# An inverse transform table built later and two groups of additions issued earlier, in a state-space and SwiGLU block kernel

## The chip, the cores and the metric

The kernel runs on one core of one Trainium2 chip. The metric is the device time of one execution, in microseconds (us); below it is called the timed value. The span in a profile, from the first to the last instruction, is about 1.8 us shorter.

## The reference

One batch of 2048 tokens with 640 channels. Condensed below. It is a block of two parts, each behind a layer norm: a state-space convolution whose kernel K is built from 192 complex exponentials per channel and applied by Fourier transform, and a SwiGLU feed-forward part with 1536 hidden channels.

```python
P = jnp.exp(logdA[:, :, None] * l[None, None, :])          # (D, N, L)
K = jnp.einsum("dn,dnl,dn->dl", Cc, P, dB).real
Yf = rfft(pad(u)) * rfft(pad(K)); y = irfft(Yf)[..., :L] + u * Dskip
...
h  = x + A(layernorm(x))
h2 = h + (silu(layernorm(h) @ w1) * (layernorm(h) @ w3)) @ w2
```

## The kernel before

Two parts of it matter.

**The building of K** (about 0 to 100 us of the span). The channels go in three chunks (256, 256 and 128). For each chunk VectorE and ScalarE make two tables, `at` and `bt`. ScalarE contributes sines, cosines and exps; VectorE multiplies them (`b_mul`). TensorE multiplies the tables (`k_mm`), ScalarE takes the product out of PSUM (`k_evac`, tile `kc`), TensorE transforms it (`k_dft`), and ScalarE takes out the result (`kf_evac`, tile `kf`). The inverse table `gt` with its negated copies is made by four transposes and four ScalarE copies; the second of these copies makes `nft`, a negated part of the forward table. `nft` is first used at 84.8 us, `gt` at 91.6 us.

```python
def inverse_table():
    tp = ps2("g", BF16)
    for i in range(NFT):
        T.transpose(out=tp[:, 0, i * P:(i + 1) * P], in_=ft[...], identity=ident[:])
    S.copy(out=gt[:], in_=tp...)          # L168
    S.mul(out=nft[:]..., mul=-1.0)        # L169
    S.mul(out=gn2[:], ..., mul=-1.0)      # L170
    S.mul(out=gn[:], ..., mul=-1.0)       # L171
...  (cut)
zs1 = z_sin(1)
at1 = a_first(1, wv1)
inverse_table()
run(a0)                                    # VectorE: end of the chain of table at, chunk 0
stg = [b_rest(0, bt0, "exp", ig) for ig in IGS]     # ScalarE: exps, L280; an exp table load comes first
for ig, st in zip(IGS, stg):
    b_mul(0, bt0, "exp", ig, st)           # VectorE: bt = bt * stg, L319
warm(14, last_a(0, at0)); warm(10, last_b(0, bt0, 1))
ze1 = z_exp(1)
bt1 = b_tile(1)
b_first(1, bt1, "exp")
ze2 = z_exp(2)
...  (cut)
pk = k_mm(0, at0, bt0, 0)                  # L373
...
k_evac(0, pk, kc, 0)
run(a_chain(1, at1, zs1))
pb = k_dft(0, kc)                          # L422
...
kf_evac(0, pb, "SSSS")                     # L439
for b in range(n_mm(1)):
    k_evac(1, k_mm(1, at1, bt1, b, (lambda: warm(6, idle, "g")) if b else None), kc, b)   # kc: L408
...
warm(6, idle)
pb = k_dft(1, kc); kf_evac(1, pb, "SSSS")
for part in range(2):
    fwd(0, SPLIT[0], part)                 # L576
...
pk = k_mm(2, at2, bt2, 0)                  # "the third chunk's k_mm"
```

`warm` issues matmuls without a use, meant to keep TensorE's clock up.

**The eight periods** (from 100 us). Each handles 256 tokens, by a string of steps that gives the program order. `Gi` is a pair of gate and up products (L853) with their evacuations `sg` and `up`, `Hi` the VectorE product of the two (L865). `I0`, `I1` are inverse transforms, `A0`, `A1` the additions that make h for the next period (L759 to L767), `T` its layer norm statistics (variance on VectorE, the power on POOL), and `X` its normalization (`xl`, L820), the store of it to DRAM (`xd`) and a DMA transpose back (`xt`). The next period's `G0` needs `xt`.

```python
PERIODS = ["p p G0 u1 p p H0 u2 u3 k G1 H1 I0 G2 H2 A0 I1 G3 H3 A1 T s0 G4 H4 s1 G5 X H5 L D s2 s3 K O0 B0 q0 q1 Y0 O1 ...", ...]
```

## Time and profile before

| | value |
|---|---|
| timed, 3 runs | 276.61 us (276.31 to 277.1) |
| the profiled execution | timed 276.8 us, span 275.0 us |
| busy share of the span: PE, DVE, ACT | 82%, 80%, 72% |
| DVE and ACT busy, 34 to 64 us (of 30 us) | 29.50 and 29.98 us |
| first gate matmul of period 0, of period 1 | 100.22 us, 122.40 us |

These are the page's engine shares, and the busy tenths of 40 slices of 6.9 us each. PEclk is the granted clock in tenths.

```profile
PE   7550165204789999999999999999999999999995
...
DVE  6999999999999989898879897797897886731112
ACT  6999999999998988856765774783693662642441
...
PEclk9555559555999999999999999999999999999999
```

VectorE and ScalarE fill the slices up to the 13th (about 86 us), TensorE those after the 14th. Next come two stretches of the first regime, from the view by windows: each engine's busy time with its count of instructions.

```profile
34.00:64.00 30.00, 10.81 (x533) 7.16 (x532) 29.50 (x35) 29.98 (x79) 0.00 (x0) 0.61 0.15 32
64.00:86.00 22.00, 17.06 (x665) 12.58 (x665) 21.41 (x41) 21.90 (x67) 3.34 (x9) 0.89 0.02 4
```

After the window and its length come PE, weight loads, VectorE, ScalarE and POOL, then the granted clock and the DMA. Only 0.5 and 0.6 us of VectorE's time are idle, and still less of ScalarE's. One of its idle stretches is in the timelines of ScalarE (first) and VectorE (second): start, duration, line, and in brackets the idle time before it and what ended it.

```profile
29.38 0.60 ACT L168 COPY gt<-ps_420 128x512 bf16<-128x512 bf16 x1
...
30.73 1.28 ACT L280 ACT_TABLE_LOAD   x1
32.02 3.42 ACT L280 ACTIVATE stg<-alp_182 128x384 bf16<-128x384 f32 x8
```

```profile
32.04 1.83 DVE L357 TENSOR_TENSOR at<-at,tt 128x1536 bf16<-128x1536 bf16 x2
34.23 2.16 DVE L319 TENSOR_TENSOR bt<-bt,stg 128x3840 bf16<-128x3840 bf16 x1 [0.36 <-ACT stg L280]
```

The four table copies (the first is shown, the last ends at 30.72) stand ahead of the exp table load, and VectorE waits 0.36 us for the exps behind it. The end of this regime, in TensorE's timeline, is the third chunk's k_mm. It waited for VectorE's last `bt`; TensorE had been idle for 0.17 us before it:

```profile
85.49 0.38 PE L576 MATMUL ps_1924<-uln_1755,nft 128*128 128x512 bf16 x1
86.04 1.96 PE L373 MATMUL ps_1934<-bt,at 128*64 128x64 bf16 x128 [0.17 <-DVE bt L319]
```

The second regime has one hole, before period 1. These are VectorE's and then TensorE's timeline, and the landing time of the one transpose in that window:

```profile
108.69 0.43 DVE L865 TENSOR_TENSOR hm<-sg,up 128x512 bf16<-128x512 bf16 x1 [0.15 <-ACT up L860]
109.03 0.32 DVE L759 TENSOR_TENSOR yt<-ys 128x320 bf16<-128x320 bf16 x1
...
111.35 0.43 DVE L865 TENSOR_TENSOR hm<-sg,up 128x512 bf16<-128x512 bf16 x1 [0.32 <-ACT up L860]
111.69 0.32 DVE L759 TENSOR_TENSOR yt<-ys 128x320 bf16<-128x320 bf16 x1
...
115.05 0.80 DVE L820 TENSOR_SCALAR xl<-xs,hmv,rs 128x640 bf16<-128x640 bf16 x2 [0.58 <-POOL rs L470]
```

```profile
121.50 0.43 PE L573 MATMUL ps_2687<-usd,ft 128*128 128x320 bf16 x2
122.40 1.26 PE L853 MATMUL ps_2710<-xt,w1sb 128*128 128x256 bf16 x10 [0.46 <-DMA xt<-xd]
```

```profile
DMA to landing us min/median/max: 3.8/3.8/3.8
```

Without the wait the gate matmul would have started at 121.77, 0.27 us after the first of two such matmuls begins; the hole is 122.40 − 121.77 = 0.63 us.

### The profile page before, as it was taken

What the parts mean: (1) busy time and instruction counts of PE and PEld (TensorE: products, weight loads), DVE (VectorE), ACT (ScalarE), POOL (GpSimd) and SP (SyncE); (2) the same over time, 40 slices, a digit from 0 to 9 for tenths busy, and PEclk for the clock granted to TensorE, in tenths of its full rate; (3) what the DMA queues carried; (4) which work ended last, traced back from release to release, by engine and by line L of the source; (5) the groups of instructions that cost most, each with busy time, mean ns of one, the idle gap of its engine ahead of it and who ended that gap; (6) DMA issues with size and microseconds to landing.
All of it is one profiled execution on the core that took longest, in us unless ns stands there. A gap on an engine that the chain in (4) does not pass through costs nothing.

```text
span 275.0 us, 7442 instructions
## 1 busy us (share of the span) xinstructions
PE 226.6 (82%) x3093; PEld 179.0 (65%) x3095; DVE 220.1 (80%) x443; ACT 199.2 (72%) x445; POOL 38.6 (14%) x78
## 2 busy tenths in 40 slices
PE   7550165204789999999999999999999999999995
PEld 6220134203556668868878878878887887887883
DVE  6999999999999989898879897797897886731112
ACT  6999999999998988856765774783693662642441
POOL 8500100000400214140140130121102100010000
PEclk9555559555999999999999999999999999999999
DMA  5761850000000699150041221131041040032001
GB/s 139 218 268 38 191 114 5 5 0 2 6 5 2 166 338 348 28 107 27 4 94 48 45 54 48 29 70 50 0 98 48 4 97 26 24 68 54 24 2 48
DMA packets 31844, 20.21 MB, mean 73 GB/s; under 512 B 20546, under 2 KB 31170, under 8 KB 31682
## 3 DMA queue, kind: packets, MB, share of 16 engines
q1 hardware_dynamic: 31250, 19.54, 26.4%
q8 instruction: 24, 0.39, 0.6%
q10 hardware_dynamic: 560, 0.20, 0.3%
q14 instruction: 10, 0.08, 0.1%
HBM read 12.26 MB, written 5.18 MB: 63 GB/s over the span
## 4 chain that ended last, share of the span: by engine, by line
PE 62%; DVE 16%; ACT 2%; DMA 1%; issue 1%; POOL 1%; DVEq 0%; ACTq 0%
DVE at L352 4%; DVE tt L354 4%; DVE at L357 4%; DMA xt<-xd 1%; DVE bt L324 1%; PE ps_4198 L879 1%; PE ps_3276 L879 1%; PE ps_4488 L879 1%; PE ps_4458 L879 1%; PE ps_4231 L879 1%; PE ps_3935 L879 1%; PE ps_3622 L879 1%; PE ps_3309 L879 1%; PE ps_2996 L879 1%; PE ps_4675 L879 1%; PE ps_3902 L879 1%
## 5 line engine op out<-in xcount | busy, mean ns | idle before, releaser
L853 PEld LDWEIGHTS <-w1sb 128*128 128x128 bf16 x480 | 46.9, 98 | 8.1 <-DMA xt<-xd 0.8
L853 PEld LDWEIGHTS <-w3sb 128*128 128x128 bf16 x480 | 47.0, 98 | 5.4
L879 PEld LDWEIGHTS <-hm 128*128 128x128 bf16 x360 | 35.2, 98 | 13.3
L865 DVE TENSOR_TENSOR hm<-sg,up 128x512 bf16<-128x512 bf16 x48 | 20.2, 422 | 22.3 <-ACT up L860 21.6
L487 ACT ACTIVATE jk<-xs 128x640 bf16<-128x640 bf16 x30 | 22.4, 747 | 0.3
L352 DVE TENSOR_TENSOR at<-at,zs 128x1536 bf16<-128x1536 bf16 (+3 forms) x30 | 20.4, 680 | 0.3
L354 DVE TENSOR_TENSOR tt<-at,zs 128x1536 bf16<-128x1536 bf16 (+3 forms) x30 | 20.2, 673 | 0.0
L357 DVE TENSOR_TENSOR at<-at,tt 128x1536 bf16<-128x1536 bf16 (+3 forms) x30 | 19.1, 679 | 0.5
L422 PEld LDWEIGHTS <-wt 32*128 32x128 bf16 (+1 forms) x512 | 9.1, 107 | 15.2 <-issue 15.2
L470 POOL TENSOR_TENSOR rs<-va,nhalf 128x2 f32<-128x2 f32 x8 | 6.4, 803 | 85.4 <-DVE va L475 85.4
L900 DVE TENSOR_TENSOR ot<-ob,xs 128x640 bf16<-128x640 bf16 x15 | 7.4, 491 | 13.5 <-ACT ob L889 13.2
L373 PEld LDWEIGHTS <-at 128*32 128x32 bf16 (+3 forms) x896 | 9.7, 102 | 10.8 <-issue 9.8
L448 PEld LDWEIGHTS <-ident 128*128 128x128 bf16 x51 | 5.7, 118 | 14.5 <-DVE at L357 6.7
L767 DVE BATCH_NORM_STATS2 hst<-xs 128x6 f32<-128x320 bf16 (+2 forms) x32 | 14.2, 485 | 0.8 <-ACT xs L749 0.4
L422 PE MATMUL ps_1122<-kc,wt 32*128 32x64 bf16 x128 | 3.5, 227 | 13.2 <-ACT kc L408 11.6
L499 POOL TENSOR_SCALAR mv<-sm 128x2 f32<-128x2 f32 (+1 forms) x8 | 3.0, 370 | 76.9 <-ACT jk L487 76.8
L709 DVE TENSOR_TENSOR xf<-z 128x1280 bf16<-128x1280 bf16 x14 | 11.6, 825 | 0.8
L373 PE MATMUL ps_536<-bt,at 128*32 128x32 bf16 (+1 forms) x512 | 5.0, 196 | 6.9 <-issue 6.9
L820 DVE TENSOR_SCALAR xl<-xs,hmv,rs 128x640 bf16<-128x640 bf16 x16 | 6.4, 444 | 4.5 <-POOL rs L470 4.5
L448 PE MATMUL ps_464<-at,ident 128*128 128x256 bf16 x14 | 3.2, 419 | 6.5 <-DVE at L357 6.5
L283 ACT ACTIVATE bt<-alp_182 128x384 bf16<-128x384 f32 x15 | 7.8, 522 | 0.0
L286 ACT ACTIVATE bt<-alp_182 128x384 bf16<-128x384 f32 x15 | 7.8, 521 | 0.0
(559 smaller groups left out, 619.3 us busy)
## 6 DMA issues: line engine op xcount, KB each, us to landing
xs<-in_A_u_dram SPq DMA_DIRECT2D x4, 640.0 KB, 5.8
out_dram<-ot SPq DMA_DIRECT2D x15, 160.0 KB, 1.8
xd<-xl SPq DMA_DIRECT2D x14, 160.0 KB, 2.4
wt<-ftd SPq DMA_DIRECT2D x4, 512.0 KB, 7.7
w2sb<-in_B_w_dram SPq DMA_DIRECT2D x1, 1920.0 KB, 14.2
w1sb<-in_B_w_dram SPq DMA_DIRECT2D x2, 640.0 KB, 8.6
w3sb<-in_B_w_dram SPq DMA_DIRECT2D x2, 640.0 KB, 7.8
w1sb<-in_B_w_dram SPq DMA_DIRECT2D x2, 320.0 KB, 4.4
```

What stands on the lines that cost most here:

```text
L352: V.tensor_tensor(out=av[:, part, :, o0:o0 + w, :], in0=src, in1=z4[:, 0].broadcast_to([P, cw // 2, w, 2]), op=ALU.mult)
L354: V.tensor_tensor(out=tv[:, part], in0=src, in1=z4[:, 1].broadcast_to([P, cw // 2, w, 2]), op=ALU.mult)
L357: V.tensor_tensor(out=dst, in0=dst, in1=tv[:, 1 - part], op=(ALU.add if part else ALU.subtract))
L373: T.matmul(pk[m * t:m * t + m, half, gi * m:gi * m + m].rearrange("p (i c) -> p i c", c=n), lhsT=at[r, c + m * t:c + m * t + m], rhs=bt[r, ...
L422: T.matmul(pp[t][:, f * n:(f + 1) * n], lhsT=wt[m * t:m * t + m, i, f * P:(f + 1) * P], rhs=kc[i // ni][m * t:m * t + m, i % ni * n:(i % n ...
L448: T.matmul(pw[:, 0, 0:n_cols], lhsT=ident[:], rhs=rhs, start=True, stop=True)
L487: S.activation(out=jk[:], in_=xs[:, 2 * c + k, :], func=(ACT.Identity, ACT.Square)[m], accum_out=st1[c][:, m, k:k + 1])
L709: V.tensor_tensor(out=x[:, :, :, r], in0=z[:, :, :, r], in1=zp[:, :, :, r], op=(ALU.add if c % 2 else ALU.subtract))
L767: V.bn_stats(out=st[:, k, int(r.start > 0), :], in_=xs[:, 2 * c + k, r])
L853: T.matmul(pg[:, b, u * TB:(u + 1) * TB], lhsT=w[:, kt, fb * P:(fb + 1) * P], rhs=xts[c][:, kt, :], start=(kt == 0), stop=(kt == DT - 1))
L865: V.tensor_tensor(out=hms[c][:, 2 * fp:2 * fp + 2, :].rearrange("p u t -> p (u t)"), in0=sg[:], in1=up[:], op=ALU.mult)
L879: T.matmul(po[:, q, 0:D // 2], lhsT=hms[c][:, fb, k * P:(k + 1) * P], rhs=w2sb[:, fb, q * (D // 2):(q + 1) * (D // 2)], start=(fb == 0), s ...
```

## The change

The intent: the inverse table and its copies are not wanted until 84.8 us, so their 1.35 us of ScalarE can come behind the exps that VectorE waits for. And the additions that lead to period 1's `xt` should not stand behind two products that wait for ScalarE.

```diff
     at1 = a_first(1, wv1)
-    inverse_table()
     run(a0)
...
     b_first(1, bt1, "exp")
+    inverse_table()
     ze2 = z_exp(2)
...
-    PERIODS = ["... G1 H1 I0 G2 H2 A0 I1 G3 H3 A1 T s0 G4 ...",
+    PERIODS = ["... G1 H1 I0 G2 A0 H2 I1 G3 A1 T H3 s0 G4 ...",
```

No instruction is added or removed. Below, the first half is called the table move, the second the new order.

## The prediction

> **What bounds the kernel now.** Three regimes. From 24 to 86 us VectorE and ScalarE bind together: in the windows 34 to 64 and 64 to 86 us VectorE is busy 29.50 of 30 and 21.41 of 22 us, ScalarE 29.98 and 21.90; TensorE 10.8 and 17.1. From 86 to 100 us a chain hops between engines. From 100.2 us TensorE binds, matmuls back to back with one hole: in the list of waits, period 1's first gate matmul (122.40 us) waits for the transposed tile xt from DMA, matmul queue 0.46 us, weight loads 0.80.
>
> **What the change does.** The instruction order shows that none is added or removed; two groups move.
>
> 1. The inverse table (four transposes, four ScalarE copies, 29.38 to 30.73 us) goes from before the exp table load to behind the 15 exps of the second chunk. In the timeline VectorE ends its chain at 33.87 us, but its next product starts at 34.23, waiting for the fifth exp (32.02 + 5 x 0.424 = 34.14). With the exps 1.35 us earlier it can start at about 33.8: VectorE gains 0.36 to 0.44 us. ScalarE gains nothing: it spends the 1.35 us later, and from 45.7 us is where it was. [...] the trace has these copies under Sin, and the instruction order shows the same loads after. The transposes then sit behind warm-up matmuls (about 42 us), before ScalarE wants them (44.4). VectorE's other inputs have slack, so the lead reaches the last multiplication of bt (85.50 us). TensorE, waiting for it (k_mm of the third chunk, 86.04), is free only at 85.71, after forward transforms that follow a DFT released by ScalarE. So 0.33 of the 0.4 us passes; period 0's product gains only 0.2 (then it waits for vt, 87.23), but is needed later. Expected: 0.33 us on everything from 88 us.
>
> 2. In period 0, A0 moves ahead of H2, A1 and T ahead of H3. Now A0 starts at 109.03 behind H2, which waited for up until 108.65; A1 sits behind H3 (idle 0.32). The variance goes to POOL at 114.22, xl starts at 115.05 after POOL's 0.80 us power, the stores to xd at 115.53, the DMA transpose at 118.56, landing about 122.35. After: A0 from 108.46, 2.0 us; H2 0.34; A1 1.9; aggregation 0.44; xl at about 114.2, 0.88 us earlier, xt about 121.5. TensorE's previous matmul lets go at 121.77, so 0.63 of the 0.88 counts. H5 stays bound to its up (115.69), before its use (about 117); three sg/up buffers cover the later H2.
>
> Later xt has slack (issued 139.49, median 3.7 us to landing, needed 144.64), and VectorE mostly follows TensorE, so the gain is kept.
>
> **Sum:** 0.33 + 0.63 = 0.96 us off 276.61: 275.7 us. 80% range 275.2 to 276.4. Faster by over 2%: 1%; within 2%: 98%; slower: 1%.
>
> **What would show it.** VectorE's 0.36 us wait for stg gone, first bt product at 33.8; third-chunk k_mm at 85.7; period 0's first gate matmul at 99.9 instead of 100.22; xl at about 113.9 (both shifts), period 1's first gate matmul at about 121.4 with no DMA wait; TensorE gapless after; span about 274.0.
>
> **What would make it wrong.** ScalarE, gapless from 24 to 87 us, might absorb the first gain; the transpose DMA might be slowed by the tail of the w2 load (14.2 us to landing, ending about 112.4); a later period might meet a new wait; run-to-run spread (276.31 to 277.1) is nearly the gain's size.

0.33 + 0.63 = 0.96 us is the whole sum.

## The result

| | before | after |
|---|---|---|
| timed, median (lowest to highest, runs) | 276.52 us (276.31 to 277.1, 4) | 276.04 us (275.74 to 276.41, 4) |
| ratio after to before | | 0.998 (95%: 0.9959 to 1.0) |
| span of the profiled execution | 275.0 us | 274.1 us |

A ratio is the mean time of one kernel's fast runs over the mean of the other's fast runs of the same rounds, so it is not quite the ratio of the medians. The value 275.7 us was expected, with a range of 275.2 to 276.4. The median lies in the range, but of the 0.96 us of gain only 0.48 us shows.

The profile after, in the same views. ScalarE and VectorE around the exps:

```profile
29.78 1.28 ACT L280 ACT_TABLE_LOAD   x1
31.07 4.24 ACT L280 ACTIVATE stg<-alp_182 128x384 bf16<-128x384 f32 x10
```

```profile
34.05 2.15 DVE L319 TENSOR_TENSOR bt<-bt,stg 128x3840 bf16<-128x3840 bf16 x1
```

The wait for `stg` is gone. The start is 0.18 us earlier, and not 0.36 to 0.44, because this execution began later: ScalarE's first exp waited for the small input `log_dt`.

```profile
3.99 0.21 ACT L177 ACTIVATE dtb<-ldc 128x5 bf16<-128x5 bf16 x1 [0.28 <-DMA ldc<-in_A_log_dt_dram]
```

In the profile before, the same instruction started at 3.72 without a wait. Counted from it, VectorE's product starts 30.51 us later in before (34.23 − 3.72) and 30.06 us later in after (34.05 − 3.99): 0.45 us gained. The moved copies (44.73 to 46.05 us in after) bring no further table load: there are four loads in each of the two profiles, and the load before the exps keeps its 1.28 us.

TensorE at the third chunk's k_mm, and around the hole; VectorE's additions; the landing of the transpose:

```profile
85.69 0.38 PE L576 MATMUL ps_1924<-uln_1755,nft 128*128 128x512 bf16 x1
86.00 1.96 PE L373 MATMUL ps_1934<-bt,at 128*64 128x64 bf16 x128
```

```profile
108.17 0.32 DVE L759 TENSOR_TENSOR yt<-ys 128x320 bf16<-128x320 bf16 x1
...
110.41 0.32 DVE L759 TENSOR_TENSOR yt<-ys 128x320 bf16<-128x320 bf16 x1
...
113.77 0.80 DVE L820 TENSOR_SCALAR xl<-xs,hmv,rs 128x640 bf16<-128x640 bf16 x2
```

```profile
121.19 0.43 PE L573 MATMUL ps_2687<-usd,ft 128*128 128x320 bf16 x2
121.46 1.25 PE L853 MATMUL ps_2710<-xt,w1sb 128*128 128x256 bf16 x10
```

```profile
DMA to landing us min/median/max: 3.2/3.2/3.2
```

The third chunk's k_mm has no VectorE wait any more; TensorE's own work sets it. `xl` is 1.28 us earlier, and period 1 begins without a hole. From profile to profile the steps are what was predicted: 121.46 us for period 1 (predicted about 121.4), 274.1 us for the span (about 274.0). So in this pair of profiles the mechanism is there. The question is why the timed gain is half of what this pair of profiles shows.

### The profile page after: what moved, and what is told of

Same layout as the page of the kernel before. It is cut to its first block, busy times and chain, and to the rows that moved or that the text cites. A ratio compares the mean times of both kernels' runs of the same rounds, so it can differ in the third digit from the quotient of the medians.

```text
span 274.1 us, 7441 instructions
## 1 busy us (share of the span) xinstructions
PE 227.6 (83%) x3093; PEld 179.7 (66%) x3095; DVE 220.0 (80%) x443; ACT 199.1 (73%) x445; POOL 38.6 (14%) x78
## 4 chain that ended last, share of the span: by engine, by line
PE 67%; ACT 29%; DMA 1%; DVE 1%; issue 0%; POOL 0%; ACTq 0%
ACT bt L286 5%; ACT bt L283 3%; ACT bt L280 2%; ACT stg L283 2%; ACT stg L280 2%; ACT kc L408 2%; ACT jk L487 1%; PE ps_1784 L422 1%; ACT zs L239 1%; PE ps_4675 L879 1%; PE ps_4488 L879 1%; PE ps_4231 L879 1%; PE ps_4198 L879 1%; PE ps_3935 L879 1%; PE ps_3902 L879 1%; PE ps_3622 L879 1%
```

## The experiments

All kernels gave correct results. In each job the kernel before was run again on the same chip. "Late" below means that ScalarE waited for TensorE in the stretch of 70 to 86 us, so TensorE and not VectorE set the time there.

### First set: the change again, its halves, and a later transpose

`e1_again` is the changed kernel unedited. `e2_table_only` and `e3_order_only` each keep one half of the diff above. `e4_x_late` takes the kernel before and issues the normalization and transpose one step later:

```diff
-    ... G5 X H5 L D s2 s3 ...
+    ... G5 H5 X L D s2 s3 ...
```

> The changed kernel, unchanged, timed again in five rounds. Theory A (both gains real, 0.33 us at the third-chunk k_mm and 0.63 us at period 1's first gate matmul; the 0.48 us of the first medians is only run-to-run spread, of which one source is how late the first DMA of log_dt lands): 0.9 to 1.2 us faster than before in the mean, ratio about 0.996. Theory B (only one of the two steps is real, or the hole before period 1 is not always there): about 0.3 to 0.6 us, ratio about 0.998. In the trace, measured from ScalarE's first activation after the log_dt load (dtb), period 1's first gate matmul comes 1.2 us earlier than before by A and by the first trace.

> Only the inverse table is moved; the period-0 order is that of before. Theory A: VectorE's wait for stg gone, third-chunk k_mm 0.3 us earlier after dtb, then 0.3 to 0.55 us earlier at period 0's first gate matmul (0.3 from the table, 0.2 more if the issue gap inside the last DFT is also gone), the hole before period 1's first gate matmul still there (matmul queue 0.46 us): 0.3 to 0.55 us faster. Theory B1 (ScalarE, which does the same work in the same time, absorbs it): 0.0 to 0.1 us.

> Only the period-0 order is changed; the table stays before the exps. Theory A: stg wait of 0.36 us still there, nothing earlier up to period 0's first gate matmul, then the hole before period 1's first gate matmul closed: 0.63 us faster. Theory B2 (the hole is given back in period 1 by another wait): about 0.0 to 0.2 us. With e2 the two should add up to e1.

> Kernel before with X (normalisation of h and the transposes' DMA) one place later, behind H5, so the opposite dose of the second step. X then starts after H5 (about 116.1 instead of 115.05 us), xt lands about 1.05 us later, and period 1's first gate matmul waits 1.05 us longer. Theory A (the gate matmul follows the landing of xt one for one as long as it is later than 121.77 us): 1.0 us slower than before. Rival (xt is hardly the limit; something else sets the start of period 1, or TensorE makes up for it): 0 to 0.4 us slower.

| run | median us (lowest to highest) | ratio to before (95%) |
|---|---|---|
| before, same job | 276.57 (276.19 to 277.95) | |
| e1_again | 276.66 (276.32 to 277.13) | 0.9997 (0.9973 to 1.0021) |
| e2_table_only | 276.64 (276.07 to 277.51) | 0.9999 (0.9974 to 1.0024) |
| e3_order_only | 276.28 (276.12 to 277.05) | 0.9982 (0.9957 to 1.0006) |
| e4_x_late | 277.47 (276.92 to 278.19) | 1.0027 (1.0003 to 1.0051) |

The gain of the whole change did not repeat here, the table move alone was worth nothing, and the new order alone 0.18%. All three intervals include 1. In the trace of e1, period 1 begins 118.21 us after the exp of `log_dt` (121.93 − 3.72), against 118.68 in before: 0.47 us earlier, where the profile after showed 1.21. Only e4 is clear of the noise: +0.75 us by the ratio (0.0027 × 276.6). In its trace `xl` is at 116.02 instead of 115.05 and period 1 at 123.03 instead of 122.40, at nearly the same start of period 0 (100.19 and 100.22). But the wait for `xt` did not grow: it is 0.46 us in both, behind the same hole of 0.63 us, because the transpose landed after 3.5 us instead of 3.8 and TensorE's work before it was later too. That work had waited for VectorE's `usd`, which stands behind `xl` on VectorE. First before, then e4:

```profile
117.67 0.43 PE L573 MATMUL ps_2651<-usd,ft 128*128 128x320 bf16 x2
```

```profile
118.20 0.84 PE L573 MATMUL ps<-usd,ft 128*128 128x320 bf16 x4 [0.40 <-DVE usd L562]
```

So e4 delayed two things at once. It shows that time lost on VectorE around `xl` reaches the end, and not that a later transpose alone does.

The trace of e2 says where the table's gain went. First ScalarE, then TensorE:

```profile
71.39 1.20 ACT L439 CAST kf<-ps 128x256 bf16<-128x256 f32 x4 [0.43 <-PE ps L422]
...
79.70 0.55 ACT L408 ACTIVATE kc<-ps,mask 128x256 bf16<-128x256 f32 x1 [0.50 <-PE ps L373]
```

```profile
86.97 1.96 PE L373 MATMUL ps<-bt,at 128*64 128x64 bf16 x128
```

ScalarE, which has no slack here, loses 0.43 + 0.50 us to TensorE, and k_mm starts at 86.97, in spite of a VectorE that had waited 0.36 us less at the start. In the profile before, these two ScalarE instructions (70.81 and 78.53 us) had no wait at all. e3 shows the same lateness (0.20 and 0.54 us, k_mm at 86.97) without the table move, so the move does not cause it. The granted clock differs between the executions: e2 had 0.50 in 64 to 72 us and 0.80 in 72 to 80 us, before had 0.69 and 1.00.

```profile
64.00:72.00 8.00, 4.74 (x263) 3.73 (x263) 7.58 (x11) 7.90 (x23) 1.70 (x5) 0.69 0.02 5
72.00:80.00 8.00, 6.79 (x269) 4.58 (x269) 7.86 (x22) 8.00 (x29) 1.64 (x5) 1.00 0.02 4
```

```profile
64.00:72.00 8.00, 4.43 (x258) 3.75 (x258) 7.58 (x11) 7.47 (x21) 1.56 (x6) 0.50 0.02 5
72.00:80.00 8.00, 7.88 (x269) 5.08 (x268) 7.86 (x21) 7.50 (x28) 1.39 (x4) 0.80 0.02 4
```

The first pair is the kernel before, the second e2. The profile after also had 0.50 in 64 to 72 us (0.92 in 72 to 80), and in it ScalarE did not wait for TensorE. This gave a theory and a rival. The clock theory (C in the expectations): the table move's gain is lost where the half clock slows the transform of chunk 0 and what follows. The rival (D): the pauses marked "issue" inside that work, in which TensorE waits for nothing that the profile shows, make it late whatever the clock.

### Second set: the clock raised ahead of the transform

`e5_before_warm` and `e6_after_warm` add 23 filler matmuls between the product and the transform of chunk 0 (the same on both kernels):

```diff
     run(a_chain(1, at1, zs1))
+    pwk = ps2()
+    T.matmul(pwk[:, 0, 0:256], lhsT=ident[:], rhs=a_view(1, at1)[:, 0, 0:32, 8:12, :], start=True, stop=True)
+    for _ in range(22):
+        T.matmul(pwk[:, 0, 0:512], lhsT=ident[:], rhs=xs[:, 12:14, 0:256], start=True, stop=True)
     pb = k_dft(0, kc)
```

> Kernel before plus 23 matmuls that feed nothing, put on TensorE between the products of the first chunk and its DFT, started when VectorE has finished the at tile up to j = 11 (about 58.2 us) and over before about 65.5 us. Theory C (formed from the traces of e1 to e4: whether the table move pays is decided by how late TensorE, at half clock, finishes the first chunk's DFT and the second chunk's products; where it is late ScalarE waits 0.4 to 1.0 us for it, and VectorE's lead is not the limit): granted clock 1.0 from about 62 us on instead of about 70 to 75, no wait of ScalarE at the kf and kc copies between 70 and 80 us, third-chunk k_mm again bound by VectorE's bt (wait 0.1 to 0.3 us), time 0 to 0.6 us below before and less spread. Rival D (the delay is the issue gap of 1.2 to 1.8 us inside that DFT, whatever the clock): the waits of ScalarE remain, time as before.

> Changed kernel with the same 23 matmuls. Theory C: with TensorE's clock made safe both steps pay, 0.3 us at the third-chunk k_mm and 0.63 us at period 1's first gate matmul, so 0.9 us below e5 and 0.9 to 1.5 us below before (ratio 0.9945 to 0.997). If the table move cannot pay even then (ScalarE's path as such is the limit), 0.6 us below e5.

Measured: e5 277.42 us (276.68 to 278.41), ratio 1.0028 (1.0009 to 1.0046); e6 277.31 us (276.43 to 277.64), ratio 1.0012 (0.9994 to 1.003); before in this job 276.85 us. e5 is slower than before; the interval of e6 includes 1. e6 is about 0.4 us below e5 (1.0028 − 1.0012), where 0.6 to 0.9 us was expected. TensorE's timeline, e2 first, then e5:

```profile
65.82 2.91 PE L422 MATMUL ps<-kc,wt 32*128 32x64 bf16 x204 [10.74 <-ACT kc L408]
70.47 0.88 PE L422 MATMUL ps<-kc,wt 32*128 32x64 bf16 x52 [1.74 <-issue]
```

```profile
65.56 1.65 PE L422 MATMUL ps<-kc,wt 32*128 32x64 bf16 x181 [0.66 <-ACT kc L408]
69.95 1.20 PE L422 MATMUL ps<-kc,wt 32*128 32x64 bf16 x75 [2.73 <-issue]
```

In the first part of the transform the fillers did what they should: 181 matmuls take 1.65 us in e5, against 204 in 2.91 us in e2 (granted clock in 66 to 68 us 1.00 and 0.50). But the pause grew from 1.74 to 2.73 us, and the transform ended at 71.15 us against 71.35, which is no more than the 0.26 us by which it began earlier. So the faster clock ahead of the transform alone did not help here, and the clock theory in this form fell. The dose was not complete: the record has full clock from 62.6 to 69.4 us and half clock from 69.4 to 72.8, so what followed the pause was slow again.

The kept traces agree with the pause as the cause of ScalarE's wait at `kf`. It had no wait where the pause took 1.18 to 1.57 us (after, e1, e7, before) and waited 0.16 to 0.47 us where it took 1.51 to 2.73 us (e3, e2, e4, e8, e6, e5). Three of the four without a wait (after, e1, e7) had half clock through 64 to 72 us. The granted clock in the records is 0.5 or 1.0, in stretches that are multiples of 3.41 us, but for the last of a trace (in before 3.41, 34.13, 6.83 and 20.48 us, then full clock to the end). What sets the stretches these traces do not show.

The pause moved in a telling way. Counted in TensorE's records (weight loads and matmuls) from the first instruction of the transform, the pause lies at 408 in before, e2, e7 and e8. With 23 fillers, each a weight load and a matmul, hence 46 instructions, it lies at 362 = 408 − 46 in e5 and e6. Other pauses lie 256 instructions apart (−616, −360, −104, 408, 664, 920 in before; the records show 663 and 919 for the last two, and with 3093 matmuls on the page against 3095 weight loads a record or two seem to be missing). On the DMA side, in the window of 60 to 80 us of the profile before, 40 slices of 0.5 us:

```profile
GB/s 0 0 0 0 0 0 0 0 0 0 0 0 0 0 0 33 0 0 16 0 0 0 33 0 0 0 0 0 0 0 33 0 0 0 0 0 0 33 0 0
...
q8 instruction: 4, 0.07, 1.4%
```

Each 33 GB/s in a slice of 0.5 us is one packet of 16 KB on the queue that the profile calls "instruction". One begins at 67.67 us in before, some 2 us after the transform starts, and TensorE goes on at about 70 us in before and in e5 alike (70.16 and 69.95). That is 2.49 us after the start of this packet in before and 2.37 us in after; over all 14 traces it was 2.3 to 3.0 us. The whole execution has 24 packets on this queue, and 24 × 256 is 6144, close to TensorE's 6188 weight loads and matmuls. So one packet for every 256 instructions fits the counts; it is read from them, and no trace shows a pause waiting for a packet. Below, a place where a pause can recur, 256 instructions from the last, is called a boundary. The pause at the second boundary after TensorE's long wait takes 1.2 to 2.7 us in the ten traces named above (1.18 us in after, 2.73 in e5).

### Third set: the pause moved out of the transform

If the count of instructions decides, extra instructions ahead of the transform move the pause out of it. `e7_before_nomid` and `e8_after_nomid` drop the six fillers in the middle of chunk 1's second product, from before and from after. `e9_after_pad_nomid` adds to e8 76 small matmuls, 152 instructions:

```diff
-        k_evac(1, k_mm(1, at1, bt1, b, (lambda: warm(6, idle, "g")) if b else None), kc, b)
+        k_evac(1, k_mm(1, at1, bt1, b), kc, b)
```

```diff
     run(a_chain(1, at1, zs1))
+    pwk = ps2()
+    for _ in range(76):
+        T.matmul(pwk[:, 0, 0:P], lhsT=ident[:], rhs=ident[:], start=True, stop=True)
     pb = k_dft(0, kc)
```

> Kernel before without the six filler matmuls (512 columns, feeding nothing) that stand inside the second half of the second chunk's products. Theory C2 (after e5 and e6: the clock is not the cause; TensorE's instruction supply fixes the end of the first chunk's DFT at about 4.3 us after its start, and what follows, fillers included, then makes the second half of the products late, for which ScalarE waits 0.2 to 1.0 us at kc): that wait is gone because 1.3 to 2.6 us of fillers are, the wait at kf of 0 to 0.47 us stays, the spread shrinks; 0.2 to 0.6 us below before. Rival (fillers keep the clock up and losing them costs): ScalarE's wait the same or longer, k_dft of the second chunk slower, time at or above before.

> Changed kernel without the same six fillers. Theory C2: with ScalarE no longer waiting at kc, VectorE's bt is what the third-chunk k_mm would wait for, so the table move pays its 0.3 us: 0.6 to 0.9 us below e7, 0.8 to 1.5 us below before. If the table move never pays: 0.5 to 0.6 us below e7.

> As e8, and 76 small matmuls (128 columns, feeding nothing) in TensorE's idle time before the first chunk's DFT, counted so that the 256-instruction blocks in which the issue gaps recur (indices 408, 664, 920 after the DFT's first instruction in the trace of before) begin exactly at the DFT: no issue gap inside the DFT, its end 1 to 1.5 us earlier (about 69.5 us), ScalarE's wait at kf gone, 0.2 to 0.4 us below e8. Rival (the gaps follow elapsed time or memory traffic, not the count): the gap stays inside the DFT, time as e8.

"Instruction supply" in the first of these is the reading of the pauses: TensorE went on 4.39 us after the start of the transform in e5 and 4.08 us in e6. No trace shows the supply itself. That fillers keep the clock up was a rival to be tested.

| run | median us (lowest to highest) | ratio to before (95%) |
|---|---|---|
| before, same job | 276.64 (276.29 to 277.24) | |
| e7_before_nomid | 276.38 (276.2 to 277.25) | 0.9995 (0.9981 to 1.0009) |
| e8_after_nomid | 276.08 (275.72 to 276.98) | 0.9981 (0.9966 to 0.9997) |
| e9_after_pad_nomid | 276.78 (276.62 to 278.06) | 1.0013 (0.9996 to 1.003) |

e7 was expected 0.2 to 0.6 us below before and is 0.1 us below by the ratio, with an interval that includes 1. e8 was expected 0.5 to 0.9 us below e7 and is about 0.4 us below.

e9 bears out the count theory. Its transform, of 512 instructions, runs without a pause. The boundaries, moved by 152, are now at 256 = 408 − 152 and at 512; the first is crossed without a pause, as the one at 152 was in before, and the pause comes at the second, behind the transform. (In e9 the profile puts this pause, 1.45 us, down to VectorE's `bt`; in e10 and e11 of the next set, which have the same 512 instructions ahead of it, it is marked "issue", 1.21 and 1.07 us. In these and in e12 the transform runs without a pause too.)

```profile
65.68 3.25 PE L422 MATMUL ps<-kc,wt 32*128 32x64 bf16 x256 [4.31 <-ACT kc L408]
...
85.64 1.96 PE L373 MATMUL ps<-bt,at 128*64 128x64 bf16 x128
```

ScalarE's `kf` and the second `kc` have no wait, k_mm starts at 85.64, and period 0 at 99.64 us, the earliest of all runs. And yet the timed value is no better. Period 1 begins at 121.83, behind a new hole (the gate matmul stands on L856 here, as the edit added three lines):

```profile
120.89 0.43 PE L573 MATMUL ps<-usd,ft 128*128 128x320 bf16 x2
121.83 1.26 PE L856 MATMUL ps<-xt,w1sb 128*128 128x256 bf16 x10 [0.51 <-DMA xt<-xd]
```

```profile
xt<-xd SPq DMA_TRANSPOSE x1, 4.8
```

The transpose took 4.8 us to land instead of 3.2. In this trace one of the 16 KB instruction packets falls inside the transpose (at 119.06 us, within 117.0 to 121.8); in the other traces of the first three sets none does. That is a coincidence in one trace. It was not tested. Part of e9's time also lies outside the profile: its span of 274.4 us is that of e8, and its profiled execution was timed 0.45 us longer (276.62 and 276.17).

e7 settles more than it was built for. Its `xl` starts at the same time as in before (115.04 and 115.05), and period 0 too (100.21 and 100.22), but the transpose landed after 3.2 us instead of 3.8:

```profile
121.49 0.43 PE L573 MATMUL ps<-usd,ft 128*128 128x320 bf16 x2
121.81 0.94 PE L853 MATMUL ps<-xt,w1sb 128*128 128x256 bf16 x7
```

```profile
DMA to landing us min/median/max: 3.2/3.2/3.2
```

So with the old order and a fast transpose the hole is 121.81 − 121.49 − 0.27 = 0.05 us, and the span is 274.4 us against 275.0. The 0.63 us that the new order saves in the profile before are not there when the transpose lands early.

### Fourth set: the halves, with the fillers made as short as can be

To have TensorE early in every execution, `e10_before_fill`, `e11_order_fill` (new order alone) and `e12_after_fill` drop the middle fillers and place tiny matmuls (32 columns) so that the pauses fall elsewhere: 76 ahead of chunk 0's transform, and 54 with four fillers instead of six ahead of chunk 1's.

```diff
     run(a_chain(1, at1, zs1))
+    pwa = ps2()
+    for _ in range(76):
+        T.matmul(pwa[0:32, 0, 0:32], lhsT=ident[:, 0:32], rhs=ident[:, 0:32], start=True, stop=True, tile_position=(0, 0))
     pb = k_dft(0, kc)
...
-    warm(6, idle)
+    pwb = ps2()
+    for _ in range(54):
+        T.matmul(pwb[0:32, 0, 0:32], ...)      # as above
+    for _ in range(4):
+        T.matmul(pwb[:, 1, 0:512], lhsT=ident[:], rhs=idle, start=True, stop=True)
     pb = k_dft(1, kc)
```

> Kernel before with TensorE made early on purpose: 76 tiny matmuls (32 columns) before the first chunk's DFT, so that instruction blocks begin at it; no fillers inside the second chunk's products; and 54 tiny ones (in place of two fillers) before the second chunk's DFT, so that from there on the blocks fall where they did (in e9 a block's 16 KB instruction load began at 119.06 us, inside the xt transpose, which took 4.8 us to land instead of 3.2 to 3.8). Theory C3: no ScalarE wait at kf and kc between 70 and 80 us; VectorE keeps its 0.36 us wait for stg and its bt sets the third-chunk k_mm (wait 0.2 to 0.6 us in weight loads); hole before period 1 of 0.05 to 0.65 us, as xt lands in 3.2 to 3.8 us. Time 0.2 to 0.6 us below before.

> The same fillers with the period-0 order of the change, table still before the exps. Theory C3: same as e10 up to period 0's first gate matmul, no hole before period 1 (xt in 3.2 to 3.8 us): 0.3 to 0.6 us below e10. If the hole is there again, the transposes' landing and not the order decides it.

> The same fillers with the whole change. Theory C3 (the table move pays once TensorE is not what ScalarE waits for): no stg wait, third-chunk k_mm and period 0's first gate matmul 0.3 us earlier after dtb than in e10 and e11, 0.3 us below e11 and 0.6 to 0.9 us below e10, 0.9 to 1.4 us below before (ratio 0.995 to 0.997). Rival (ScalarE's own path absorbs the table move even then): equal to e11.

| run | median us (lowest to highest) | ratio to before (95%) |
|---|---|---|
| before, same job | 276.37 (276.09 to 277.24) | |
| e10_before_fill | 277.48 (276.85 to 278.82) | 1.0041 (1.0018 to 1.0064) |
| e11_order_fill | 277.22 (276.43 to 277.55) | 1.0019 (1.0002 to 1.0036) |
| e12_after_fill | 277.26 (276.69 to 277.74) | 1.0022 (1.0006 to 1.0039) |

This set failed as a construction. All three are slower than before, and TensorE is late again, this time by my own edit: the 54 tiny matmuls make chunk 1's transform start at 81.0 to 81.3 us instead of 80.3 in the profile before. ScalarE's last `kf` then waits 0.29, 0.29 and 1.50 us for TensorE; in e12 the clock was half from 79.6 to 83.0 us besides. What the set shows of the two halves with a late TensorE is weak: e11 is about 0.6 us below e10 by the ratios (1.0041 − 1.0019), but the two intervals overlap, e10 had three runs of the group with the lower recorded clock (see below) and e11 one, and in the other group the means differ by 0.14 us (277.12 and 276.98). In e10's own trace the hole is only 0.08 us. e12 against e11 shows no gain of the table move (1.0022 and 1.0019).

### All runs together, by clock

Nearly every run carries its mean granted clock, and the runs fall into two groups, with means of about 0.89 to 0.90 and of 0.94 to 0.96. The page's row of clocks suggests that in the second group the clock is full from the start:

```profile
PEclk9999999555599999999999999999999999999999
```

This is e2, of the second group; the kernel before, shown at the start, is of the first. But the row misleads. The trace of e2 has no record of the clock before 41.0 us, and the row shows full clock where there is none. The matmuls tell: the same instruction takes 0.23 us in before and 0.29 us in e2, and in before its like takes 0.29 us too once half clock is on record (at 8.70 us). First before, then e2:

```profile
4.97 0.23 PE L200 MATMUL ps_206<-dg,par_ar 128*128 128x128 bf16 x1
```

```profile
5.04 0.29 PE L200 MATMUL ps<-dg,par_ar 128*128 128x128 bf16 x1
```

So in the first group (before, after, e4, e7) the clock is full for 3.4 us from about 4 to 5 us on, then half to about 42 us, full to about 49, and half to 69 to 73 us. In the second (e1, e2, e3, e8) it is half from the start to between 41 and 44 us, full to about 48, and half to about 75 us, in e8 with one full stretch of 3.4 us before the end. The mean of 0.95 comes from the missing records; counted with half clock before the first record, I estimate 0.88 for e2 and 0.89 for before. That the runs without a profile are of the same two kinds is inferred from their means.

The traces also show what goes with the two kinds. All stretches lie on a grid of 3.41 us. A line of the grid falls 0.66 to 1.79 us after the start of the span in the eight traces with the early full stretch (before, after, e4, e5, e6, e7, e9, e12), and outside this, 2.53 to 3.41 or 0.06 to 0.41 us after it, in the six without (e1, e2, e3, e8, e10, e11). No run set this position, so it is a regularity of 14 traces and not a tested cause.

In the profiles of the first group (before, after, e4, e7) the clock granted in 72 to 80 us was 0.92 to 1.00, in those of the second (e1, e2, e3, e8) 0.79 to 0.83. These are the mean times of the groups, over all jobs (a grouping made after the runs, not planned; the number of runs in brackets; e4, e9 and the kernels of the second and fourth sets are left out; the clock is the recorded mean):

| kernel | first group (about 0.89 to 0.90 on record) | second group (0.94 to 0.96 on record) |
|---|---|---|
| before | 276.49 us (22) | 276.90 us (23) |
| after, with e1_again | 276.27 us (6) | 276.68 us (4) |
| e2_table_only | 276.62 us (1) | 276.76 us (5) |
| e3_order_only | 276.32 us (2) | 276.43 us (4) |
| e7_before_nomid | 276.37 us (4) | 276.88 us (2) |
| e8_after_nomid | 276.15 us (4) | 276.21 us (2) |

Two things follow. An execution of before in the second group is 0.4 us slower (276.90 − 276.49). The likely reason, argued and not tested, is that its half clock lasts further into the stretch where TensorE's work matters. It does not hold for every program: in the fourth set it is the first group that is slower (e10: 278.26 us, 3 runs, against 277.12, 3 runs). And within a group the whole change is worth about 0.2 us in both; the standard errors of the small groups are about 0.2 us, so this is an estimate and no more. Of the four runs that gave 276.04 us, three were in the first group; the clocks of the runs of before beside them are not on record, so whether that flattered the change is not known.

The whole change was in fact compared five times within one job, each time against its like without it. By the ratios it gained 0.55 us (the first result), 0.1 (e1 against before), 0.4 (e6 against e5), 0.4 (e8 against e7) and 0.5 (e12 against e10). The weighted mean from the run times is 0.35 us, with a standard error of about 0.12 us. The new order alone gained 0.5, 0.1 and 0.6 us (e3 against before, e1 against e2, e11 against e10). The table move alone gained nothing: 0.0, −0.4 and −0.1 us (e2 against before, e1 against e3, e12 against e11), each within its noise.

## Why the prediction was right or wrong

**The time and the class: right.** 275.7 us with a range of 275.2 to 276.4 was expected, 276.04 measured, within 2% of before. But the gain, predicted at 0.96 us, was 0.48 us in the first result, 0.1 us (0.0003 of the time) in its repetition, and about 0.2 us within a clock group. Between 0.1 and 0.6 us is what the five comparisons support together (0.35 us with a standard error of 0.12); most of them alone are not told apart from nothing. That the median fell into the range is in part luck: in the repetition (e1) the changed kernel took 276.66 us, outside the range.

**"VectorE gains 0.36 to 0.44 us": right.** The wait for `stg` is gone, and the product comes 0.45 us earlier, counted from the exp of `log_dt`. That exp's own start lies between 3.62 (e5) and 3.99 us (after) in the traces; where it is latest, it waited for its input.

**"0.33 us on everything from 88 us": not borne out as a mean.** This is the first mis-sized term of the sum. The prediction looked for TensorE's next claim in one trace and found 85.71 us, so 0.33 us passed. In the profile after k_mm is TensorE-bound at 86.00, which is 0.31 us earlier counted from the exp of `log_dt`. But the slack itself was smaller: where TensorE sets k_mm, it starts 0.31 us after the last forward matmul begins (after, e1, e2, e3), which in before is 85.80 us (85.49 + 0.31), so 0.24 us was VectorE's; the rest came from TensorE being 0.07 us earlier in after. In other executions TensorE is later than that by itself: 86.28 us in e1, 86.97 in e2 and e3, 86.24 in e4, 86.25 in e8. VectorE's lead then ends in a wait for TensorE or, by way of ScalarE, for the next exps. Two things can make TensorE late, and both vary between executions or with the program: pauses of up to 2.7 us at boundaries of 256 instructions (that the count sets their place is shown by e5 and e9, which moved them by 46 and 152), and the half clock that lasts to about 69 to 75 us. That the clock contributes rests on the groups of runs, not on an experiment; e5, which raised the clock, did not help. The prediction named ScalarE as the place where the gain could be absorbed; it is, but what ScalarE waits for there is TensorE. That the table move pays once TensorE is early was not shown by any run: the set built for it (e10 to e12) failed.

**"0.63 of the 0.88 counts": right for that profile, the upper end as a mean.** This is the second mis-sized term. The shift of `xl` was as predicted, and in seven of the eight traces with the new order the hole is gone, with landings of 3.2 to 3.8 us (in e9, with 4.8, it is not). But the hole it removes depends on the landing in the old order: 0.63 us with 3.8 (before), 0.64 with 3.8 (e2), 0.41 with 3.6 (e5), 0.05 with 3.2 (e7), 0.08 with 3.2 (e10). The prediction took 122.35 us for the landing from one profile and treated it as fixed.

**The pair of profiles.** The profile before was of an execution of 276.8 us, slower than the mean of its clock group (276.49) and with a late transpose. The profile after was of one of 275.85 us, faster than its group's mean (276.27) and with an early one. Their difference of 0.95 us matches the prediction, and it is not the difference of the kernels.

**Sum.** Table move: 0.33 us at most, and no gain in three comparisons of run times. New order: between 0.05 and 0.64 us by the holes in the traces. The gain of about 0.35 us that the runs show fits, and 0.96 us was the sum of two upper ends.

**Left open.** Why the transpose takes 3.2 us in one execution and 3.8 in another; whether an instruction packet inside it made it 4.8 in e9; whether the position on the grid of 3.41 us decides between the two clock histories, as it seems from the 14 traces; and the table move's mean worth, which the times do not resolve below about 0.2%.

**The best version** is e8, the whole change without the six fillers in the middle of chunk 1's product: 276.08 us against 276.64 of before in the same rounds (ratio 0.9981, interval below 1). Beside the changed kernel, 276.04 us in another job, it is not shown to be better; and the fillers alone (e7) are not clear of nothing.

## What to carry to other kernels

A wait read from one profile is one draw: before its length goes into a sum, look whether it hangs on something that varies between executions, such as a DMA's landing (here 3.2 to 4.8 us for one transpose) or the clock (here half to 69 us in before and to 75 us in e2), and count the part that is there in most of them. When two engines are both nearly full (here 29.50 and 29.98 of 30 us) and a third is a few tenths of a microsecond behind, look what the third does before counting on work taken from the first: here VectorE's lead was 0.45 us in after, k_mm still started at 86.97 us in e2, where TensorE was late, and no gain showed in the run times. For gains below the spread of the runs, compare runs of like clock, check the recorded clock against the duration of like matmuls (here 0.23 us at full and 0.29 at half clock), and repeat the result before explaining it.
